# Two heads to a load and longer runs of wo in a decode attention kernel that waits for memory

## The chip, the cores and the metric

One core of one Trainium2 chip. The metric is device time in microseconds (us). Executions vary by about 0.3%, and a few are over 1.5% longer than the fastest of their kernel ("slow"); only fast ones are compared.

## The reference, cut to what matters

A decode step for one token: sliding-window attention (32 heads, a window of 4096 keys, head size 128, bf16), gated by a small MLP.

```python
W = min(4096, max(256, Sk // 4))                  # 4096 of Sk = 32768
q = (x @ wq).reshape(...)                         # 32 heads of 128
k, v = k_cache[:, :, Sk - W:, :], v_cache[:, :, Sk - W:, :]
p = softmax(einsum("bhqd,bhkd->bhqk", q, k) * Dh ** -0.5)
s = einsum("bhqk,bhkd->bhqd", p, v).reshape(...) @ wo
g = silu(mlp(x))       # [...] w2 multiplies the hidden row shifted along a sequence of length 1: zeros
return x + s * g
```

A head needs 1 MB of keys and 1 MB of values, so 67.1 of the 78.85 MB read are keys and values.

## The kernel before

Each head's keys, and each head's values, are one DMA of 128 partitions x 8 KB, issued by SP (the engine that starts the loads here) in program order. Even heads take their scores on DVE, the vector engine (multiply, then reduce); odd heads are transposed on PE, the matmul engine, copied out by ACT, the scalar engine, and multiplied on PE. Values follow keys by four heads (`LAG`). Keys and values each have a ring: a set of buffers that the loads fill in turn (`K_BUFS`, `V_BUFS`).

```python
K_BUFS = 12
V_BUFS = 7
...
def load_kv(pool, cache, h):
    t = pool.tile([P, NC, Dh], BF16, tag="kv", name="kv")          # NC = 32, Dh = 128: 8 KB a partition
    load(t[:], cache[0, h, W0:, :].rearrange("(p c) d -> p c d", p=P))
    return t
...
blocks = [(0, 8), (8, 8), (16, 8), (24, 4), (28, 4)]
...
def load_wo(i):
    ...
    if n == 8:
        t = k_pool.tile([P, n, D], BF16, tag="kv", name="wo_8")
    else:
        t = v_pool.tile([P, n, D], BF16, tag=f"wo{i}", bufs=1, name="wo_4")
...
for i in range(H + LAG):
    if i < H:
        k_head(i, load_kv(k_pool, A_k_cache, i))
    if i == LAG:                                   # the weights' space becomes the value ring
        wts_guard.__exit__(None, None, None)
        v_pool = ctx.enter_context(tc.tile_pool(name="v", bufs=V_BUFS))
    if i >= LAG:
        v = load_kv(v_pool, A_v_cache, i - LAG)
        ...                                        # load_wo(i) when its block is next
        v_head(i - LAG, v)
```

## Time and profile before

| | before |
|---|---|
| time, median of the first 3 runs | 198.67 us |
| span in the profile | 196.8 us |
| read from memory | 78.84 MB |
| rate from 34 to 187 us | 424 GB/s |
| loads on SP | 76 |
| packets on SP's queue | 11176 |

In the strips of the profile each column is a fortieth of the span: on the DMA line the busy tenths of the sixteen DMA engines, below it the GB/s they moved. A queue (q1 carries the loads, q8 the instruction fetches) has its packets, MB and share of the engines' time. In a timeline the columns are start and duration in us, engine, line, operation, tiles, sizes and count, then in brackets the idle time of the engine ahead of them and what ended it. The prediction shows the lines themselves.

### The profile page before, as it was taken

The numbers are of one execution on the slowest core, as the hardware profiler recorded it, in microseconds if no ns is written. First come the engines' busy times: TensorE is split into PE (matmuls) and PEld (weight loads), VectorE is DVE, ScalarE is ACT, GpSimd is POOL, SyncE is SP. The second block draws the span as 40 slices with busy tenths as digits, with TensorE's granted clock in tenths as the row PEclk, the third lists the DMA queues.
The fourth block names the chain that finished last, engine by engine and source line by source line (L and its number), as shares of the span: only waits on it lengthen the run. The fifth ranks groups of instructions, "written<-read, shape, count | busy, mean of one in ns | idle before, by whom it ended". The sixth has DMA issues, their size and how long they took to land.

```text
span 196.8 us, 5237 instructions
## 1 busy us (share of the span) xinstructions
PE 119.4 (61%) x2399; PEld 108.4 (55%) x2399; DVE 126.9 (64%) x140; ACT 69.3 (35%) x82; POOL 4.9 (3%) x17
## 2 busy tenths in 40 slices
PE   0315896851969474684829293756665654929443
PEld 0314745841969473583829292656565653929332
DVE  1225049998959993959387937959198929594301
ACT  2000329742565243070707070242525250707000
POOL 1011000000000000000000000000000000000000
PEclk9999999695585555576766667555555585575555
DMA  6999899999999999999999999999999999999960
GB/s 185 383 485 446 355 416 421 426 426 421 426 421 423 421 421 425 423 425 420 426 421 428 421 425 416 425 420 426 423 428 423 425 418 425 421 426 422 426 268 10
DMA packets 11349, 79.17 MB, mean 402 GB/s; under 512 B 1376, under 2 KB 1984, under 8 KB 2368
## 3 DMA queue, kind: packets, MB, share of 16 engines
q1 hardware_dynamic: 11176, 78.85, 96.3%
q8 instruction: 18, 0.29, 0.6%
q10 hardware_dynamic: 152, 0.00, 0.0%
q14 instruction: 3, 0.02, 0.0%
HBM read 78.84 MB, written 0.00 MB: 401 GB/s over the span
## 4 chain that ended last, share of the span: by engine, by line
DMA 71%; DVE 12%; issue 6%; PE 6%; ACT 2%; POOL 1%; SPq 0%; POOLq 0%
DMA kv<-in_A_v_cache_dram 40%; DMA kv<-in_A_k_cache_dram 30%; DVE sS L265 7%; DVE prod L262 3%; ACT kt L272 1%; PE a_ps L202 1%; PE qT_ps L221 1%; PE oT L364 1%; PE qb_ps L230 1%; PE h_ps L135 1%; PE y_ps L135 0%; PE ln_ps L140 0%; PE ln_ps L152 0%; ACT q_bc L232 0%; POOL ln_rstd_x L158 0%
## 5 line engine op out<-in xcount | busy, mean ns | idle before, releaser
L272 ACT COPY kt<-pt 128x1024 bf16<-128x1024 bf16 x64 | 60.2, 1025 | 73.0 <-PE pt L271 73.0
L265 DVE TENSOR_REDUCE sS<-prod 128x32 f32<-128x4096 bf16 x16 | 70.7, 4419 | 0.5
L271 PE MATMUL pt<-ident_bf,kv 128*128 128x128 bf16 x512 | 53.8, 298 | 18.2 <-DMA kv<-in_A_k_cache_dram 17.7
L271 PEld LDWEIGHTS <-kv 128*128 128x128 bf16 x512 | 49.8, 140 | 19.7 <-DMA kv<-in_A_k_cache_dram 18.7
L364 PEld LDWEIGHTS <-kv 128*128 128x128 bf16 x1024 | 30.0, 102 | 30.5 <-DMA kv<-in_A_v_cache_dram 22.8
L262 DVE TENSOR_TENSOR prod<-kv,q_bc 128x4096 bf16<-128x4096 bf16 x16 | 36.5, 2283 | 11.0 <-DMA kv<-in_A_k_cache_dram 8.8
L364 PE MATMUL oT<-pT,kv 128*128 128x1 bf16 x1024 | 32.6, 165 | 17.6 <-DMA kv<-in_A_v_cache_dram 17.3
L243 PE MATMUL sT<-qT_bf,kt 128*128 128x1 bf16 x512 | 20.4, 166 | 2.6 <-ACT kt L272 2.3
L243 PEld LDWEIGHTS <-kt 128*128 128x128 bf16 x512 | 18.3, 103 | 3.4 <-ACT kt L272 3.2
L300 PE MATMUL den_ps<-pT,ones_bf 128*128 128x128 bf16 x8 | 2.0, 253 | 16.9 <-ACT pT L294 16.9
L371 DVE TENSOR_TENSOR o<-oT,rden 128x4 bf16<-128x4 f32 x7 | 1.1, 162 | 17.3 <-PE oT L364 17.3
L294 ACT ACTIVATE pT<-e 128x128 bf16<-128x128 f32 x8 | 2.5, 309 | 16.5 <-DVE e L290 16.5
L140 PEld LDWEIGHTS ln_ps<-x_f,ones_f 128*128 128x128 f32 x4 | 1.0, 312 | 11.3 <-DVE x_f L182 6.4
L287 POOL PARTITION_ALL_REDUCE mb<-m x8 | 3.0, 373 | 162.5 <-DVE m L285 162.5
L205 ACT ACTIVATE a_bf<-a_ps 128x10 bf16<-128x10 f32 x1 | 0.2, 180 | 17.4 <-PE a_ps L202 17.4
L302 DVE TENSOR_REDUCE den<-den_ps 128x4 f32<-128x128 f32 x8 | 2.3, 292 | 5.5 <-PE den_ps L300 5.5
L135 PEld LDWEIGHTS <-ox 128*1 128x1 bf16 x112 | 2.5, 113 | 5.3 <-DVE ox L341 5.3
L367 DVE TENSOR_TENSOR o<-oT,rden 128x1 bf16<-128x1 f32 x4 | 0.6, 161 | 7.2 <-PE oT L364 7.2
L230 PE MATMUL qb_ps<-wq_sb,xn_rep 128*128 128x512 bf16 x16 | 5.2, 497 | 0.0
L135 PE MATMUL y_ps<-wo,ox 128*1 128x128 bf16 x112 | 3.7, 306 | 2.3 <-DVE ox L341 2.3
L140 PE MATMUL ln_ps<-x_f,ones_f 128*128 128x4 f32 x4 | 1.2, 365 | 5.9 <-DVE x_f L163 4.9
L290 DVE TENSOR_TENSOR e<-sS,mb 128x64 f32<-128x64 f32 x8 | 1.8, 224 | 3.9 <-POOL mb L287 3.9
(79 smaller groups left out, 48.2 us busy)
## 6 DMA issues: line engine op xcount, KB each, us to landing
kv<-in_A_k_cache_dram SPq DMA_DIRECT2D x32, 1024.0 KB, 19.7
kv<-in_A_v_cache_dram SPq DMA_DIRECT2D x32, 1024.0 KB, 19.7
wq_sb<-in_A_wq_dram SPq DMA_DIRECT2D x1, 4096.0 KB, 19.2
wo<-in_A_wo_dram SPq DMA_DIRECT2D x3, 1024.0 KB, 20.4
w_sb<-in_B_w_dram SPq DMA_DIRECT2D x1, 1376.0 KB, 7.9
w_sb<-in_B_w_dram SPq DMA_DIRECT2D x1, 1024.0 KB, 10.2
w_sb<-in_B_w_dram SPq DMA_DIRECT2D x1, 512.0 KB, 3.7
wo<-in_A_wo_dram SPq DMA_DIRECT2D x1, 512.0 KB, 19.8
```

The source lines that it names most:

```text
L135: nc.tensor.matmul(ps[32 * j:32 * j + 1, :], lhsT=col, rhs=w[0:k, j * P:(j + 1) * P], start=False, stop=last, skip_group_check=True)
L140: nc.tensor.matmul(ps[:], lhsT=ones_f[:], rhs=src_f, start=True, stop=True)
L230: nc.tensor.matmul(qb_ps[:], lhsT=xn_rep[:, c, :], rhs=wq_h[:, c, 2 * i:2 * i + 8:2, :], start=(c == 0), stop=(c == KC - 1))
L243: nc.tensor.matmul(sT[:, hl // 2, c:c + 1], lhsT=kt[:, c, :], rhs=qT_bf[:, h:h + 1], start=True, stop=True)
L262: nc.vector.tensor_tensor(out=prod[:], in0=kn[:], in1=q_bc[:, h // 2:h // 2 + 1, :].to_broadcast([P, NC, Dh]), op=ALU.mult)
L265: nc.vector.tensor_reduce(out=s["sS"][:, hl // 2, :], in_=prod[:], axis=AX.X, op=ALU.add)
L271: nc.tensor.transpose(pt[:, i, :], kn[:, b * 8 + i, :], ident_bf[:])
L272: nc.scalar.copy(out=kt[:, b * 8:(b + 1) * 8, :], in_=pt[:])
L287: nc.gpsimd.partition_all_reduce(mb[:], m1[:], channels=P, reduce_op=ReduceOp.max)
L294: nc.scalar.activation(out=pT[:], in_=e[:], func=ACT.Exp, scale=scale)
L302: nc.vector.tensor_reduce(out=den[:], in_=den_ps[:], axis=AX.X, op=ALU.add)
L364: nc.tensor.matmul(oT[:, k:k + 1], lhsT=v[:, c, :], rhs=s["pT"][:, hl % 2, hl // 2, c:c + 1], start=(c == 0), stop=(c == NC - 1))
```

## The change

Keys and values are loaded two heads to a DMA (2 MB); the last two value heads stay single. The rings hold 6 and 3 such pairs. The first 16 heads of wo become one load whose runs are 16 KB. The intent: fewer, larger transfers.

```diff
-K_BUFS = 12
-V_BUFS = 7
+K_BUFS = 6
+V_BUFS = 3
[...]
+    def load_kv(pool, cache, h, split):
+        if h % 2 == 0:
+            t = pool.tile([P, 2, NC, Dh], BF16, tag="kv", name="kv")
+            pair[pool] = t
+            if h < split:
+                load(t[:].rearrange("p h c d -> p h (c d)"),
+                     cache[0, h:h + 2, W0:, :].rearrange("h (p c) d -> p h (c d)", p=P))
+        t = pair[pool][:, h % 2]
+        if h >= split:
+            load(t, cache[0, h, W0:, :].rearrange("(p c) d -> p c d", p=P))
         return t
[...]
+    make_masks(16)
[...]
-    blocks = [(0, 8), (8, 8), (16, 8), (24, 4), (28, 4)]
+    blocks = [(0, 16), (16, 8), (24, 4), (28, 4)]
[...]
-        if n == 8:
-            t = k_pool.tile([P, n, D], BF16, tag="kv", name="wo_8")
+        if n == 16:
+            t = k_pool.tile([P, n, D], BF16, tag="kv", name="wo_16")
[...]
-            k_head(i, load_kv(k_pool, A_k_cache, i))
+            k_head(i, load_kv(k_pool, A_k_cache, i, H))
[...]
-            v = load_kv(v_pool, A_v_cache, h)
+            v = load_kv(v_pool, A_v_cache, h, H - 2)
```

More of the change, by code (lines that the diff above doesn't have):

```diff
@@ L90 @@
     load(wq_sb[:], A_wq.rearrange("(p c) n -> p c n", p=P))
-    def load_kv(pool, cache, h):
-        t = pool.tile([P, NC, Dh], BF16, tag="kv", name="kv")
-        load(t[:], cache[0, h, W0:, :].rearrange("(p c) d -> p c d", p=P))
+    pair = {}
+    def load_kv(pool, cache, h, split):
[8 more added lines that the diff above has]
+            load(t, cache[0, h, W0:, :].rearrange("(p c) d -> p c d", p=P))
         return t
@@ L261, in k_head @@
             prod = prod_pool.tile([P, NC, Dh], BF16, tag="prod", name="prod")
-            nc.vector.tensor_tensor(out=prod[:], in0=kn[:],
+            nc.vector.tensor_tensor(out=prod[:], in0=kn,
                                     in1=q_bc[:, h // 2:h // 2 + 1, :].to_broadcast([P, NC, Dh]),
@@ L315, in load_wo @@
         rows = A_wo[h0 * P:(h0 + n) * P, :]
-        if n == 8:
-            t = k_pool.tile([P, n, D], BF16, tag="kv", name="wo_8")
+        if n == 16:
+            t = k_pool.tile([P, n, D], BF16, tag="kv", name="wo_16")
         else:
-            t = v_pool.tile([P, n, D], BF16, tag=f"wo{i}", bufs=1, name="wo_4")
+            t = v_pool.tile([P, n, D], BF16, tag=f"wo{i}", bufs=1, name="wo_8")
         wo_blk[i] = t
```

## The prediction

> **What bounds the kernel now.** I read the page first: the busy shares of the engines, the strip of forty slices, the chain that ended last. No compute engine is full (DVE is busiest, with 64% of the span), while the transfers are:
>
> ```profile
> DMA  6999899999999999999999999999999999999960
> GB/s 185 383 485 446 355 416 421 426 426 421 426 421 423 421 421 425 423 425 420 426 421 428 421 425 416 425 420 426 423 428 423 425 418 425 421 426 422 426 268 10
> ...
> q1 hardware_dynamic: 11176, 78.85, 96.3%
> q8 instruction: 18, 0.29, 0.6%
> ...
> DMA 71%; DVE 12%; issue 6%; PE 6%; ACT 2%; POOL 1%; SPq 0%; POOLq 0%
> ```
>
> From the second slice to the last but two the sixteen DMA engines are in the top class nearly always, and the chain hangs on landings of keys and values. So I ask: is the queue ever short of work (then deeper or earlier loads help), or does it always have work (then only fewer bytes, less cost per packet, or a better balance of the sixteen engines helps)? I narrowed the DMA view to the steady part, then asked what the issuing queue SP waits for, then its issues in order of time.
>
> ```profile
> DMA packets 8956, 64.80 MB, mean 424 GB/s; under 512 B 991, under 2 KB 998, under 8 KB 1126
> ...
> q1 hardware_dynamic: 8938, 64.53, 100.5%
> ```
>
> ```profile
> SPq L74 <- DMA kv<-in_A_v_cache_dram: 59.4, 28, 3.3
> SPq L74 <- DMA kv<-in_A_k_cache_dram: 59.2, 28, 2.9
> ...
> SPq L74 <- PE pt L271: 1.5, 5, 0.3
> ...
> SPq L74 <- PE oT L364: 0.5, 2, 0.3
> ```
>
> ```profile
> 82.67 0.33 SPq L74 DMA_DIRECT2D kv<-in_A_k_cache_dram  x1
> 85.10 0.33 SPq L74 DMA_DIRECT2D kv<-in_A_v_cache_dram  x1
> 87.52 0.33 SPq L74 DMA_DIRECT2D kv<-in_A_k_cache_dram  x1
> 90.02 0.33 SPq L74 DMA_DIRECT2D kv<-in_A_v_cache_dram  x1
> ```
>
> From 34 to 187 us the engines are full (100.5%; packet times overlap a little) at 424 GB/s. SP needs 0.33 us for an issue and does one each 2.47 us. It waits for an earlier load to land, almost never for a buffer (waits for PE are 0.3 us at most). A load lands 19.7 us after its issue, and 8 x 2.47 = 19.8: eight loads, 8 MB, are always under way. Thus the queue never runs dry, and SP's waits cost nothing.
>
> The last view is the end, in stretches of 1 us (columns: stretch, length, five engines' busy us, clock, DMA share, GB/s):
>
> ```profile
> 187.00:188.00 1.00, 0.84 (x32) 0.94 (x32) 0.11 (x1) 0.00 (x0) 0.00 (x0) 0.50 0.99 400
> 188.00:189.00 1.00, 0.16 (x6) 0.07 (x3) 0.16 (x1) 0.00 (x0) 0.00 (x0) 0.50 0.88 351
> 189.00:190.00 1.00, 0.53 (x20) 0.54 (x21) 0.00 (x0) 0.00 (x0) 0.00 (x0) 0.50 0.58 224
> 190.00:191.00 1.00, 0.48 (x19) 0.40 (x15) 0.16 (x1) 0.00 (x0) 0.00 (x0) 0.50 0.58 202
> 191.00:192.00 1.00, 0.07 (x2) 0.07 (x3) 0.00 (x0) 0.00 (x0) 0.00 (x0) 0.50 0.24 85
> 192.00:193.00 1.00, 1.00 (x40) 0.98 (x44) 0.02 (x1) 0.00 (x0) 0.00 (x0) 0.50 0.12 41
> ```
>
> The engines don't finish together. The sixteen completion increments of the last value head are 4.7 us apart (1.8 us at 50 us), and the spread grows in steps when a 16 KB instruction fetch (about 1.05 us each) occupies one engine. The shares sum to 3.4 us of full work, so balanced engines would end at 190.4 and not near 193. That is the only loss at the end, and the change doesn't aim at it.
>
> **What the Trainium skill says.** "DMA: Bandwidth & Descriptors", Rules for kernel authors, asks for 128 partitions and at least 1 MiB per DMA: the loads before fulfil it already. The same page, Where 436 GB/s comes from, puts the ceiling at 435 GB/s; the trace has 424, so all overhead of packets and loads together is 2.5%. The same page, Why a DMA increments its semaphore by 16 and not by 1, has each engine end its share with a descriptor that adds one to the semaphore. The trace agrees: 76 loads on SP x 16, the output's 4 + 4, and 152 of the two small loads on ACT make 1376, the page's number of packets under 512 B.
>
> **The change part by part.** The trace records every packet with size and duration. Medians: 4 bytes (the completion) 9 ns, 4096 bytes 159 ns, 8192 bytes 309 ns, 32768 bytes (wq) 1213 ns. From the last two, 24576 bytes take 904 ns, or 27.2 GB/s per engine; 8192 bytes at that rate take 301 ns, so a packet costs about 8 ns over its bytes.
>
> 1. Paired loads. Keys go from 32 loads to 16; values from 32 to 17 (15 pairs, heads 30 and 31 single). The runs remain 8 KB, so the packets with data are the same in number and size: only completions vanish. With wo (six loads to five) there are 76 - 44 = 32 loads fewer, on each engine 32 x 9 ns = 0.29 us.
> 2. wo in 16 KB runs. Two loads of 8 packets of 8 KB per engine become one of 8 packets of 16 KB: 8 packets fewer x 8 ns = 0.06 us.
> 3. SP issues fewer instructions: 32 x 0.33 us = 10.6 us of a queue that has 2.1 of each 2.47 us to spare. Worth nothing.
> 4. One more key head is issued ahead of the first value load, which waits until 30.1 us for the weights' space. By my sum of the slices, 11.2 MB had landed at 29.5 us of the 12.8 MB issued then, so the queue was not empty before either. Nothing.
> 5. Compute. Four more small DVE operations for the masks of 16 (0.1 to 0.3 us each by the 8's), one repack fewer but one four times as large: under 1 us of DVE, beside transfers. DVE needs per pair 2.28 + 4.42 us plus about 1 us of softmax, 7.7 us against 9.9 us of transfers for two key and two value heads. Nothing on the path.
> 6. Bytes are the same, 78.85 MB.
>
> Sum on the path: 0.29 + 0.06 = 0.35 us, so 198.67 - 0.35 = 198.3 us.
>
> **The rivals.**
> - *A load costs more than its completion packet shows.* A load of 1 MB is 65536 bytes per engine, 2426 ns at the whole rate of the 32 KB packets; it takes about 2470. At most 44 ns are the load's own, if the packets' share were nothing: 32 x 44 = 1.4 us, 196.9 to 197.3. Against it: the 8 ns per packet, times 8, already fills it.
> - *Rings.* Pairs free a buffer only when both heads are used, and three pairs of values replace seven heads. When value pair m lands, five pairs are queued behind it, or 24.7 us. Its release takes about 7 us: 1 us of products, four ACT copies at 1.03 us and the transposes if the odd key head comes between on PE, 1 us more. Some 17 us of queue are left. At the start, the fourth value pair needs V0 and V1, which were used at 50.5 us before; 26.4 MB are issued by then, which last until about 65. I expect SP's waits to move from landings to PE, without a gap. If I am wrong by 3 us in each of 15 pairs, it would be 240.
> - *HBM order.* Consecutive runs of an engine now alternate between two heads 8 MiB apart. "DMA: Bandwidth & Descriptors", Latency and other measured facts, lists copies at half[...] of the rate with a power-of-two pitch between all partitions. Here partitions stay 8 KB apart and only two heads alternate; no run shows this yet. One per cent on the 62 MB loaded in pairs is 1.5 us; more than 2.6% would make it slower by 2%.
> - *The end.* Keys 30 and 31 land together, 6.5 MB before the last value, then values 26 and 27 together. Before, PE ran V26 (174.65) ahead of K31's transposes (177.13). If that order stays, K31 waits for the pair, about 179.4 us; transposes, copies, scores and softmax (m at 182.53 to V28's product at 185.89 before, so 3.4 us) put V28 near 189.3 and the last product 0.7 to 1.0 us late: 199.2. If the keys go first there is no loss.
> - *Balance.* A fetch on another engine, or one more on the late one, moves the end by 0.6 to 1.4 us either way.
>
> **Range and chances.** The path gives 198.3. Downward the first rival reaches 197; upward the end and the balance 199.5. So 8 in 10 lie in 197.2 to 199.5. Faster by 2% (under 194.7) would need more than the whole imbalance or all overhead gone: 0.03. Slower by 2% (over 202.6) takes the HBM order or a starving ring: 0.04. Within 2%: 0.93.
>
> **What would show it.** Packets on q1 should fall by 32 x 16 + 128 = 640 to 10536 with the same MB. The steady rate should stay at 424 to 426 GB/s, issue-to-landing should rise to 22 to 29 us, and SP should wait for PE's products (the value ring) where it waited for landings. The 8 KB packet should stay near 309 ns; the 16 KB packet near 611. Slices below 415 GB/s in the middle would prove the rings guilty, longer 8 KB packets the HBM order; a wait of DVE or PE after the last key pair with a last product later than the last landing, the end. A gain over 1 us in a steady rate near 430 GB/s would mean that the load's own cost was undersized.

## The result and the profile after

The changed kernel takes 198.63 us (median of 6 runs, 198.44 to 199.49), the kernel before 198.74 us in the same rounds. The ratio is 1.0001, with a 95% interval of 0.9981 to 1.002: the same. A ratio here is the mean time of one kernel's fast runs over the mean of the other's fast runs in the same rounds, so it is not quite the ratio of the medians.

The page of the changed kernel, in the lines that answer to those of before:

```profile
DMA  6999899999999999999999999999999999999960
GB/s 189 391 439 459 373 414 414 423 424 423 426 426 424 426 424 426 421 426 424 423 424 426 439 409 419 428 423 428 423 428 424 423 423 424 421 424 423 426 241 8
...
q1 hardware_dynamic: 10536, 78.84, 96.1%
```

The strip of busy tenths is the same, and the packets fell to exactly the 10536 that were foretold. Over 34 to 187 us the DMA view still has 424 GB/s. What SP waits for did change (columns: who waited for whom, us in total, times, longest):

```profile
SPq L74 <- DMA kv<-in_A_v_cache_dram: 37.5, 10, 9.8
SPq L74 <- PE oT L375: 25.8, 11, 5.4
...
SPq L74 <- DVE m L296: 6.9, 1, 6.9
SPq L74 <- DVE prod L273: 6.0, 2, 4.8
```

Waits for keys and values to land fell from 118.6 us to 37.5 us, and waits for buffers (PE's products of values, some DVE operations) appeared. The rest of SP's spare time went to a place that I had not foreseen, the issues themselves. The timeline of SP (start, duration, then the instruction):

```profile
94.72 8.71 SPq L74 DMA_DIRECT2D kv<-in_A_k_cache_dram  x1
104.92 3.17 SPq L74 DMA_DIRECT2D kv<-in_A_v_cache_dram  x1
108.14 6.94 SPq L74 DMA_DIRECT2D kv<-in_A_k_cache_dram  x1
```

An issue of keys or values took 0.33 us before (median; at most 1.16 us); here some last up to 8.71 us. My reading is that the issue holds SP until the queue has room for its 256 packets. Two runs described below fit it. With two value pairs in the ring, so that fewer loads are under way, the longest issue of the same pairs is 0.47 us, so it is not the size of the load. With loads of 1 MB in 4 KB runs, 256 packets too, an issue takes 2.3 us (median), up to 4.7 us, so it is not the bytes either. An estimate, from the landing time over the time of one load: some 1000 packets with data are under way in the kernel before and with two value pairs, some 1500 in the changed kernel. No run isolates the limit. A key pair lands 32.5 us after its issue begins and a value pair 28.4 us after, so the queue is at least as deep as before. All of this is SP's waiting, and the engines stay full through it. The end, again in stretches of 1 us:

```profile
188.00:189.00 1.00, 0.87 (x32) 0.86 (x31) 0.08 (x1) 0.00 (x0) 0.00 (x0) 0.50 0.76 309
189.00:190.00 1.00, 0.75 (x29) 0.74 (x27) 0.16 (x1) 0.00 (x0) 0.00 (x0) 0.50 0.60 236
190.00:191.00 1.00, 0.38 (x15) 0.29 (x11) 0.16 (x1) 0.00 (x0) 0.00 (x0) 0.50 0.55 194
191.00:192.00 1.00, 0.26 (x10) 0.27 (x11) 0.00 (x0) 0.00 (x0) 0.00 (x0) 0.50 0.17 51
192.00:193.00 1.00, 0.75 (x29) 0.74 (x26) 0.16 (x1) 0.00 (x0) 0.00 (x0) 0.50 0.11 36
```

The sixteen engines again come in one after another; the completion increments of the last value head are 4.9 us apart (4.7 before).

### The profile page after: what moved, and what is told of

Its sections match the earlier page's. It is cut to its first block, busy times and chain, and to the rows that moved or that the text cites. A ratio compares the mean times of both kernels' runs of the same rounds, so it can differ in the third digit from the quotient of the medians.

```text
span 196.9 us, 5187 instructions
## 1 busy us (share of the span) xinstructions
PE 121.6 (62%) x2398; PEld 108.8 (55%) x2398; DVE 126.3 (64%) x141; ACT 69.3 (35%) x82; POOL 6.9 (3%) x17
## 3 DMA queue, kind: packets, MB, share of 16 engines
q1 hardware_dynamic: 10536, 78.84, 96.1%
## 4 chain that ended last, share of the span: by engine, by line
DMA 73%; DVE 14%; ACT 4%; PE 4%; SPq 2%; POOL 1%; issue 1%; DVEq 0%; ACTq 0%
DMA kv<-in_A_k_cache_dram 61%; DMA wo<-in_A_wo_dram 10%; DVE sS L276 9%; DVE prod L273 4%; ACT kt L283 4%; SPq L74 2%; DMA x_bf<-in_A_x_dram 2%; PE oT L375 2%; POOL mb L298 1%; PE pt L282 1%; PE sT L254 0%; PE y_ps L145 0%; DVE e L301 0%; DVE y L415 0%; DVE out_row L417 0%
## 5 line engine op out<-in xcount | busy, mean ns | idle before, releaser
L282 PEld LDWEIGHTS <-kv 128*128 128x128 bf16 x512 | 50.2, 142 | 34.9 <-DMA kv<-in_A_k_cache_dram 34.0
L375 PE MATMUL oT<-pT,kv 128*128 128x1 bf16 x1024 | 29.1, 164 | 4.4 <-DMA kv<-in_A_v_cache_dram 3.9
L375 PEld LDWEIGHTS <-kv 128*128 128x128 bf16 x1024 | 28.0, 100 | 6.3 <-DMA kv<-in_A_v_cache_dram 4.7
L254 PE MATMUL sT<-qT_bf,kt 128*128 128x1 bf16 x512 | 21.0, 166 | 11.5 <-ACT kt L283 10.9
L298 POOL PARTITION_ALL_REDUCE mb<-m x8 | 4.9, 613 | 159.8 <-DVE m L295 159.8
L240 PE MATMUL qb_ps<-wq_sb,xn_rep 128*128 128x512 bf16 x16 | 6.1, 565 | 0.0
L242 ACT CAST q_bc<-qb_ps 128x512 bf16<-128x512 f32 x4 | 2.3, 585 | 5.8 <-PE qb_ps L240 5.8
## 6 DMA issues: line engine op xcount, KB each, us to landing
kv<-in_A_k_cache_dram SPq DMA_DIRECT2D x16, 2048.0 KB, 32.5
kv<-in_A_v_cache_dram SPq DMA_DIRECT2D x15, 2048.0 KB, 28.4
```

The source lines that it names most:

```text
L240: nc.tensor.matmul(qb_ps[:], lhsT=xn_rep[:, c, :], rhs=wq_h[:, c, 2 * i:2 * i + 8:2, :], start=(c == 0), stop=(c == KC - 1))
L242: nc.scalar.copy(out=q_bc[:, i:i + 4, :], in_=qb_ps[:])
L254: nc.tensor.matmul(sT[:, hl // 2, c:c + 1], lhsT=kt[:, c, :], rhs=qT_bf[:, h:h + 1], start=True, stop=True)
L282: nc.tensor.transpose(pt[:, i, :], kn[:, b * 8 + i, :], ident_bf[:])
L298: nc.gpsimd.partition_all_reduce(mb[:], m1[:], channels=P, reduce_op=ReduceOp.max)
L375: nc.tensor.matmul(oT[:, k:k + 1], lhsT=v[:, c, :], rhs=s["pT"][:, hl % 2, hl // 2, c:c + 1], start=(c == 0), stop=(c == NC - 1))
```

## The experiments

The theory: the time is bytes, plus a little for each packet and each load, on queues that never run dry. The rivals: a load costs more than that and something else lost the gain; or the rings took back what the loads gave. All runs gave correct results. Unless said otherwise, ratios are to the kernel before in the same rounds (it had medians of 198.77 to 198.85 us there).

### Pairs without the change to wo

```diff
-    make_masks(16)
[...]
-    blocks = [(0, 16), (16, 8), (24, 4), (28, 4)]
+    blocks = [(0, 8), (8, 8), (16, 8), (24, 4), (28, 4)]
[...]
-        if n == 16:
-            t = k_pool.tile([P, n, D], BF16, tag="kv", name="wo_16")
+        if n == 8:
+            t = k_pool.tile([P, n, D], BF16, tag="kv", name="wo_8")
```

> The changed kernel with wo loaded as before, in blocks of 8 heads with 8 KB runs; keys and values stay in pairs. Theory (the time is bytes plus about 8 ns a packet plus 9 ns a completion): 0.06 us longer than the changed kernel, so 198.4 to 198.9 and a ratio to before of 0.998 to 1.002. Rival (pairing gains something and the 16 KB runs of wo lose it again, or the other way round): a ratio outside 0.996 to 1.004.

Measured: 198.67 us, ratio 0.9989 (0.9953 to 1.0026), steady rate 424 GB/s. There is no gain in one part that the other loses, as far as half a per cent shows.

### What a packet costs: 4 KB runs

On the kernel before; keys and values are reordered alike, so softmax and sum come out the same.

```diff
-        load(t[:], cache[0, h, W0:, :].rearrange("(p c) d -> p c d", p=P))
+        load(t[:].rearrange("p (b c) d -> p b (c d)", b=2),
+             cache[0, h, W0:, :].rearrange("(b p c) d -> p b (c d)", b=2, p=P))
```

> The kernel before with each key and value head read in 4 KB runs (two per partition) in place of 8 KB; same loads, same bytes. Theory (a packet costs about 8 ns over its bytes: 159 ns for 4 KB, 309 ns for 8 KB): 64 heads x 8 more packets per engine x 9 ns = 4.6 us more, 203.3 us, ratio 1.023. Rival (the packet is free and the load as a whole carries the overhead): 198.7, ratio 1.000.

Measured: 201.04 us, ratio 1.0107 (1.0068 to 1.0146). The DMA view from 34 to 187 us:

```profile
DMA packets 16171, 63.99 MB, mean 418 GB/s; under 512 B 981, under 2 KB 981, under 8 KB 15769
...
q1 hardware_dynamic: 16153, 63.72, 101.8%
```

A packet does cost, but the 4.6 us were twice too many. Measured are 2.2 us for 64 x 8 = 512 more packets on each engine, or 4.3 ns each (2.6 to 5.7 by the interval). The recorded durations (159 and 309 ns) are as foreseen, but packets overlap: the share is 101.8% here, 100.5% before. My reading of these two shares is that a part of each packet's 8 ns lies under its neighbour.

### What a load costs

First attempt, on the kernel before: two loads of 64 partitions.

```diff
-        load(t[:], cache[0, h, W0:, :].rearrange("(p c) d -> p c d", p=P))
+        src = cache[0, h, W0:, :].rearrange("(p c) d -> p c d", p=P)
+        load(t[0:64], src[0:64])
+        load(t[64:P], src[64:P])
```

> The kernel before with each key and value head loaded by two DMAs of 64 partitions; packets of data unchanged, 64 loads more. Theory (a load costs each engine only its 9 ns completion): 0.6 us more, 199.3 us, ratio 1.003. Rival (a load costs up to 44 ns beyond its packets): 2.8 us more, 201.5, ratio 1.014. If a queue of eight loads of 0.5 MB is too short: far more, with gaps in the DMA strip.

Measured: 306.59 us in its one fast run, the others up to 327.25 us (slow). The DMA view from 34 to 187 us (of a slow run, so only its order of size counts):

```profile
DMA packets 5446, 35.86 MB, mean 234 GB/s; under 512 B 1078, under 2 KB 1078, under 8 KB 1078
...
q1 hardware_dynamic: 5435, 35.70, 101.2%
```

This measures something else. The engines are busy without gaps, but an 8 KB packet takes 541 ns (median) in place of 309 ns. The Trainium skill, "SBUF — State Buffer", Door 1: The DMA port swizzle, says that partitions 0 to 63 lie behind only 8 of the 16 ports. A rate of 234 GB/s, 55% of 424, agrees. The load's own cost stayed open, so I split the head by columns: 128 partitions, one 4 KB run each, two loads. Its packets are those of the 4 KB run above, with 64 loads more.

```diff
-        load(t[:], cache[0, h, W0:, :].rearrange("(p c) d -> p c d", p=P))
+        for b in range(2):
+            load(t[:, b * (NC // 2):(b + 1) * (NC // 2), :],
+                 cache[0, h, W0 + b * (W // 2):W0 + (b + 1) * (W // 2), :].rearrange("(p c) d -> p c d", p=P))
```

> The kernel before with each head read by two loads of 128 partitions and one 4 KB run each: the packets are those of e2 (201.04 us), with 64 loads more, and every partition takes part, which the loads of 64 partitions (e3) spoiled. Theory (a load costs its 9 ns completion): 0.6 us over e2, 201.6 us, ratio 1.014. Rival (a load costs 44 ns): 2.8 us over e2, 203.8 us, ratio 1.025. Eight loads under way are 4 MB here; if that is too short a queue, there are gaps and far more.

Measured: 201.36 us, ratio 1.0123 (1.0096 to 1.0151), steady rate 418 GB/s as with 4 KB runs in one load. The difference to that run is 0.32 us for 64 loads, or 5 ns each; the two ran in different rounds, and their intervals overlap. An estimate from the two intervals puts the cost of a load at 5 ns with 15 ns either way. That fits a completion of 9 ns, cannot be told from zero, and rules out 44 ns (203.8 us). So 32 loads fewer can give about 0.2 us, and at most 0.6 us.

### The value ring

```diff
-V_BUFS = 3
+V_BUFS = 2      # first run; second run: 1
```

> The changed kernel with two pairs of values in the ring in place of three. Theory (the queue has slack): when value pair m lands, three pairs (14.9 us) are queued behind it, and the pair is used within some 3 to 7 us, so the queue stays fed: 198.6 us, ratio 1.000, steady rate 424 GB/s. Rival (the value ring of three is already at its edge): gaps, over 203 us.

> The changed kernel with one pair of values. Theory: behind a landing value pair only one key pair (4.95 us) is queued, while the pair must be used (2 to 7 us) and the next load must start[...], and the sixteen engines are up to 3.7 us apart, so the engines go idle in each of 15 rounds: 205 to 260 us, DMA share below 90% in the steady part. Rival (the ring does not matter): 198.6 us.

Measured: two pairs 198.65 us, ratio 0.9981 (0.9949 to 1.0013), steady rate 423 GB/s. One pair 221.57 us (median of its three fast runs; the two slow ones took 224.43 and 228.27 us), ratio of fast runs 1.1109 (1.1043 to 1.1176). The strip with one pair (profiled in a slow run; read it for the holes, not for the size):

```profile
DMA  6999999949998968999989999689999999936392
GB/s 225 424 382 328 404 424 420 422 182 391 376 407 350 389 291 334 421 386 396 356 341 366 418 394 420 262 334 428 394 378 409 422 421 381 341 127 242 135 369 91
```

A ring that is too small shows as holes in the strip. The changed kernel has none, and by the run with two pairs could give up a third of its value ring.

### Bytes alone: without w2, and a surprise

The changed kernel without w2, whose input is zero, so the output is the same:

```diff
-    w2_sb = wts.tile([P, KC, D], BF16, name="w2_sb")
-    load(w2_sb[:], B_w2.rearrange("(p c) n -> p c n", p=P))
[...]
-    shifted_bf = small.tile([P, KC], BF16, name="shifted_bf")      # and the products with w2
-    x1_f = small.tile([P, KC], FP32, name="x1_f")
[...]
-    xc3, _, rstd3 = ln_stats(x1_f[:], "z3")
+    xc3, _, rstd3 = ln_stats(xn_f[:], "z3")
```

> The changed kernel without w2 and the products with it. Their input is the shifted hidden row, which is all zero for a sequence of one, so the output is the same. Theory (only bytes count): 0.524 MB at 424 GB/s are 1.24 us, so 197.4 us, ratio 0.994. Rival (the start is bound by the chain of small operations and not by transfers, or the end by something other than the queue): under 0.5 us of gain.

Measured: 199.08 us, ratio 1.0002 (0.9967 to 1.0036). The theory seemed to fall. But the steady part was slower:

```profile
DMA packets 8283, 64.22 MB, mean 420 GB/s; under 512 B 520, under 2 KB 525, under 8 KB 653
```

By the packet records, an 8 KB packet averaged 313.7 ns (over those between 300 and 330 ns, here and below), in place of 310.2 ns in the changed kernel. Comparing the compiled programs, I saw that two small tiles had vanished and every key and value buffer lay 64 bytes lower in its partition. Two runs test that place: one without w2 but with 64 bytes of padding, and the changed kernel with w2 and 448 bytes of padding, which gives its buffers the remainders of 512 bytes of the disappointing run.

```diff
+    pad = small.tile([P, 16], FP32, name="pad")      # second run: [P, 112]
+    nc.gpsimd.memset(pad[:], 0.0)
```

> The run without w2 (e4) gained nothing although 0.52 MB were gone: its 8 KB packets took 313.7 ns on average in place of 310.2, and its steady rate was 420 GB/s in place of 424. Without w2 two small tiles vanish, and every key and value buffer lies 64 bytes lower in its partition: keys start at a multiple of 128 bytes (128 over a multiple of 512), in the changed kernel at 192 over one. Here 64 bytes of padding put every buffer back. Theory (the place of the buffers costs the rate): packets at 310.2 ns, 424 GB/s, and the 1.24 us of gain appear: 197.4 us, ratio 0.994. Rival (something else came with w2's removal, or that run's chip memory was slower): 313 ns and 198.9 us again.

> The changed kernel with w2 and with 448 bytes of padding, which puts all key and value buffers at the same remainders of 512 bytes as in the run without w2 (keys 128, values 192). Theory (place of the buffers): packets at about 313.7 ns, 420 GB/s, 1% of 150 us or 1.5 us more: 200.1 us, ratio 1.007. Rival: 310.2 ns and 198.6 us.

Measured: without w2, padded, 197.2 us, ratio 0.9919 (0.9893 to 0.9945). With w2 and the shift, 200.64 us, ratio 1.0091 (1.0062 to 1.012). The DMA view from 34 to 187 us, first of the padded run without w2:

```profile
DMA packets 8425, 64.89 MB, mean 424 GB/s; under 512 B 525, under 2 KB 592, under 8 KB 720
```

then of the shifted run with w2:

```profile
DMA packets 8275, 64.22 MB, mean 420 GB/s; under 512 B 515, under 2 KB 515, under 8 KB 643
```

So the padded kernel gets its gain back (packets 310.2 ns), and the changed kernel loses as much merely by moving (313.6 ns). That the place of the tiles in the partition costs 1% is shown, in both directions. To see which tiles matter, the last run moved only what lies at the end of the partition, from DVE's product tile `prod` on, 64 bytes up from the padded run:

```diff
+    vpad = prod_pool.tile([P, 16], FP32, tag="vpad", name="vpad")
+    nc.gpsimd.memset(vpad[:], 0.0)
```

> The kernel of e8 (no w2, keys at 192 over a multiple of 512 bytes, values at 256 over one; 197.2 us) with 64 bytes of padding behind the key buffers, so that only the value buffers move, to 320 over a multiple of 512. If each load is slowed by its own buffer's place, then value packets lose what they lost in e9 if 64 over a multiple of 128 is bad for them, and key packets do not: half of e9's loss, some 0.9 us, 198.1 us, a steady rate near 422 GB/s, with 8 KB packets that swing between 309 and 314 ns with a period of 10 us. If the keys' place alone decides: 197.2 us and 424 GB/s. If any odd 64 among values slows everything: 198.9 us and 420 GB/s. I expect the first, without certainty.

Measured: 199.32 us, ratio 1.001 (0.997 to 1.0051), about 2 us lost, and packets of 313.8 ns throughout. My first guess missed, and the third alternative held: with the keys where they were, moving the values (and with them `prod`, the weights, which lie in that space earlier, and the later blocks of wo) slows the packets of the whole steady part.

```profile
DMA packets 8284, 64.18 MB, mean 419 GB/s; under 512 B 522, under 2 KB 531, under 8 KB 659
```

Where the buffers start, as the remainder of the address in the partition over 512 bytes:

| kernel | keys at | values at | 8 KB packet, mean ns | steady GB/s |
|---|---|---|---|---|
| before | 320 | 0 | 310.1 | 424 |
| changed | 192 | 256 | 310.2 | 424 |
| without w2, padded | 192 | 256 | 310.2 | 424 |
| without w2 | 128 | 192 | 313.7 | 420 |
| changed, shifted | 128 | 192 | 313.6 | 420 |
| without w2, values moved | 192 | 320 | 313.8 | 419 |

The fast kernels have their values at a multiple of 256 bytes and the slow ones do not. But `prod` has the same remainder as the values in every one of these kernels, so the times alone do not tell the two apart. The packet records do, in stretches where one kind of load is alone (mean ns of an 8 KB packet):

| stretch | under way | three fast kernels | three slow kernels |
|---|---|---|---|
| 24 to 30 us | keys alone | 313.2 to 314.3 | 313.4 to 314.0 |
| 50 to 170 us | keys and values | 309.9 to 310.0 | 313.6 to 313.8 |
| 182 to 187 us | values alone; DVE is done with `prod` | 309.0 | 313.6 to 313.8 |

So the values' own place costs, without `prod` in use. And the keys, which start at no multiple of 256 in any of these kernels (128, 192 and 320 were tried), are slow in all of them while they are alone. The Trainium skill, "DMA: Bandwidth & Descriptors", How a descriptor splits into AXI transactions, says that a descriptor that does not start at a multiple of 256 bytes fetches bytes that it does not use. Both stretches with one kind of load agree with that, though the page speaks of bytes that are fetched, and what moved here is where they are written. It does not explain the mixture: in the fast kernels keys and values together take 310 ns, nearer to the 309.0 of the values than to the middle of the two. Why is open. No run had keys at a multiple of 256 bytes as well, so that it is their place that slows the keys is argued, not shown. What such a run could gain, as an estimate from 309.0 ns in place of 310.2, is 0.4% of the steady part, some 0.6 us.

### More bytes

The changed kernel with w1 loaded too (never used), in the space of the weights, so that no key or value buffer moves:

```diff
+    w1_sb = wts.tile([P, KC, D], BF16, name="w1_sb")
+    load(w1_sb[:], B_w1.rearrange("(p c) n -> p c n", p=P))
     wq_sb = wts.tile([P, KC, HD], BF16, name="wq_sb")
```

> The changed kernel with one load more, w1 (0.524 MB in 4 KB runs, never used), ahead of wq; no buffer of keys or values moves. Theory (only bytes and packets count): 0.524 MB at 424 GB/s are 1.24 us more, 199.9 us, ratio 1.006. Rival (the early part is bound by something else): 198.6 us.

Measured: 199.77 us, ratio 1.0073 (1.0031 to 1.0114), 424 GB/s, packets of 310.2 ns. That is 1.1 us over the changed kernel's 198.63 (1.4 us by the two ratios), where 1.24 was expected. With the padded run without w2 (1.4 us under it) this brackets the changed kernel: half a megabyte more or less moves the time by what the rate says, and 32 loads fewer do not.

### More instructions

```diff
-        for c in range(NC):                                           # scores of odd heads
+        for c in [c for c in range(NC) for _ in range(2)]:
[...]
-        for c in range(NC):                                           # products of values
+        for c in list(range(NC)) * (1 if i == last_block else 2):
```

> The changed kernel with each matmul of the scores done twice (the second overwrites with the same value) and each product of values done twice for the first 28 heads (the second restarts the sum): same output, the same loads, 1408 matmuls more, so 2816 instructions more on PE, or 11 fetches of 16 KB. Theory (a fetch holds one of the sixteen engines for about 1.1 us and the end waits for the slowest engine): 0.75 us more if they spread evenly, 0.4 to 2.5 us in all, so 199.0 to 201.1 us, 29 fetches of 16 KB in the trace. Rival (fetches are hidden): 198.6 us. PE has about 38% of the span free for the 20 us more.

Measured: 205.37 us, ratio 1.0328 (1.0288 to 1.0369), with 29 fetches of 16 KB. The expectation missed, and the experiment does not decide what it was made for. At the end, PE runs the last value heads back to back and waits no more for landings:

```profile
194.65 1.01 PE L375 MATMUL oT<-pT,kv 128*128 128x1 bf16 x32
195.92 0.99 PE L375 MATMUL oT<-pT,kv 128*128 128x1 bf16 x32 [0.25 <-DVE o L378]
```

The transfers have all but ended by 194 us (the DMA share is 0.20 from 193 to 194 us, then 0.02), and four heads of 1.24 us each follow. The doubled work near the end made PE the bound there. The spread of the engines rose to 6.2 us near the end of the steady part, which fits fetches that hold single engines, but what they cost in time stays open.

## Why the prediction was right

- **The bound.** A queue that never runs dry: shown. The steady rate was 424 GB/s before and after; bytes moved the time by their rate in both directions, and loads did not. Two slips in the reading of SP's waits and of the skill changed nothing: before the first value load SP did wait 7.7 us for PE (`qb_ps`, the weights' space), and the 2.5% of overhead is an estimate from the page's 435 GB/s, with which the 8 of 309 ns in the trace agree.
- **Loads.** The 640 packets fewer came out exactly. The 9 ns of a completion fits the 5 ns found, within its 15 ns either way. The rival of 44 ns a load is ruled out by the column halves.
- **Packets of wo.** The 16 KB packet took 611 ns, as foretold. The step that was mis-sized is the 8 ns saved per packet: packets overlap, and 4.3 ns are what one costs in time. The term is 0.03 us and not 0.06, and with 5 ns a load the sum is about 0.2 us, not 0.35. Neither can be told from zero by these runs, whose interval is 0.2% wide on each side. The medians differ by 0.11 us. The range held because these terms are small, not because their sum was measured.
- **SP's issues.** "Worth nothing" held, but the 10.6 us of SP's time were not saved: the fewer issues take longer.
- **Rings.** No gap, as worked out. Even two value pairs are enough, and one pair is not. By the prediction's own sign, a slice below 415 GB/s, one slice in the middle of the strip (409, after one of 439) would have convicted the rings wrongly. It lies where the 16 KB packets of wo pass (109 to 117 us), the three slices from 108.3 to 123 us average 424, and the kernel with pairs but without those packets has no such slice. SP's waits moved to PE only in part. I had foreseen landings of 22 to 29 us; keys take 32.5 us, in which the issue itself is counted.
- **HBM order.** 8 KB packets stayed at 309 ns (median); alternating between two heads costs nothing here. (The 62 MB of the prediction are 62 heads, so 65 MB; its 1.5 us and 2.6% are right for these.)
- **The end.** Keys 31 went ahead of values 26 on PE, so the loss of up to 1 us did not come. In order of time from PE's timeline of the changed kernel:

```profile
174.68 3.59 PE L282 MATMUL pt<-ident_bf,kv 128*128 128x128 bf16 x32 [2.80 <-DMA kv<-in_A_k_cache_dram]
...
179.86 1.84 PE L375 MATMUL oT<-pT,kv 128*128 128x1 bf16 x64
```

- **Balance.** The spread at the end was 4.9 us for 4.7 us: neither gained nor lost.
- **Luck.** The prediction had no word on where buffers lie. The change moved all of them, and the values happened to land on a multiple of 256 bytes again. At a bad place it would have been some 1% slower (200.64 us in the run with the shift), still within its "same" but outside its range of 197.2 to 199.5.

The best version found is the changed kernel without w2 and with 64 bytes of padding: 197.2 us, 0.8% under the kernel before.

## What to carry to other kernels

When the DMA engines are full and SP waits only for landings, ask what each transfer costs the engines, not what it costs the issuer: loads of 1 MB made into 2 MB save so little each (5 ns by the runs, with 15 either way) that the time does not show it, while half a megabyte less saves over a microsecond. Before a small change is called useless, compare the mean packet and the steady rate as well as the time: a shift of all buffers by 64 bytes hid a gain of the same size. In these runs the buffers of the values had to start at a multiple of 256 bytes of their partition for the full rate. An experiment that splits a load must keep all 128 partitions in each part.

## What the Trainium skill lacked or had wrong

- "DMA: Bandwidth & Descriptors", Rules for kernel authors: at least 1 MiB per DMA is enough here. The page's table of rates by size is for loads issued from GpSimd, and its stream of loads from SP is of one size, 1 MiB; no figure says what a larger load brings to a queue on SP that always has work. From 1 MB to 2 MB the ratio was 1.0001 here, and a load costs about 5 ns on each engine, which cannot be told from zero.
- "DMA: Bandwidth & Descriptors", How a descriptor splits into AXI transactions, gives no time, and does not say whether its multiple of 256 bytes holds for where a load writes. A shift of the value buffers by 64 bytes off that multiple took the steady rate from 424 to 419 GB/s and an 8 KB packet from 310.2 to 313.8 ns. Keys off the multiple took 313 to 314 ns alone, but 310 ns together with values on it.
- "Perfetto Trace Analysis", DMA Instruction — HWDGE (DVE, Sync), shows an issue that lasts until its descriptors are generated, but no duration and no limit of the queue: 0.33 us with eight loads of 1 MB under way, up to 8.71 us with pairs of 2 MB.
